# Four edits of order in a sigmoid-attention and SwiGLU kernel: a whole-row load, later transposes, scores ahead of FFN1, and visits moved by one tile

## The chip, the core and the metric

The kernel runs on one core of a Trainium2 chip. The core has five engines that run side by side and wait for each other through semaphores: TensorE (PE in the profile, with its weight loads shown apart as PEld), VectorE (DVE), ScalarE (ACT), GpSimd (POOL) and SyncE (SP). SP, ACT and POOL can each issue DMAs; a "q" behind an engine's name means its queue. The metric is the device time of one execution in microseconds, the median of several runs.

## The reference

```python
# q, k, v: (8 batches, 12 heads, 448 positions, 64)
scores = q @ k.T / sqrt(64) - log(448)
attn = 1 / (1 + exp(-scores)) @ v             # a sigmoid where a softmax would be
x = attn.transpose(0, 2, 1, 3).reshape(3584, 768)
g = x @ w_gate                                # (768, 1536)
out = (g * sigmoid(g) * (x @ w_val)) @ w_out  # (1536, 768), float32
```

## The kernel before, in words

**Attention.** The twelve heads of a batch are taken four at a time. Such a *quad* n (24 in all, three to a batch) has q and k, loaded as 128 rows that each hold, for two heads, 448 contiguous floats (7 chunks c of 64). They are cast to bf16 (`cast`, `cast_part`, lines 157 and 179) and transposed, on PE with a copy out of PSUM (`trans_pe`, lines 198 and 204) for quads 0 to 5 and by SP's DMA for the others. `chunk(n, c)` makes the scores of one chunk (four 64x64 matmuls, line 228) and their sigmoid on ACT (line 246, or 243 in two halves). When a quad's seven chunks are through, `pv(n)` multiplies by v (28 matmuls, line 260) and DVE copies the result out as two xT tiles (lines 269 and 274).

**Feed-forward.** FFN1 tile (b, f), one of 12 per batch, multiplies six xT pairs by w_gate and by w_val (12 matmuls, line 294). ACT takes the sigmoid of the gate half (line 312), DVE makes the product t1 (line 314) and the gated product hT (line 318). In tile f = 0 the last two pairs of both halves come last, since their xT tiles are the youngest; in every other tile the gate half is complete before the value half begins. For odd batches DVE also makes sums of hT tiles (line 377): `h_sums` puts them in a queue and `make_sums(2)` takes up to two behind each tile. FFN2 uses them in a product form with seven multiplications (`ffn2_group`, line 418) or plainly (`ffn2`, line 476).

**One ring of PSUM.** Scores, transposes, PV, FFN1 and FFN2 all draw their PSUM from one ring of four slots of two banks (`Banked`). The user four places on has to wait until the readers of a slot are done, bank by bank where the code says so.

**Order.** Everything is issued in the order of the program; no scheduler moves it. The first 30 us are written out by hand (from line 545 on): the loads, the chunks of quads 0 to 2, the transposes of quads 1 to 3 between them, PV 0 and 1, and an early start on FFN1 tiles (0, 0) to (0, 2) (`early`, from line 646), whose matmuls are put around chunks (2,5) and (2,6) and PV 2.

Quad 0's first loads are cut: ACT's queue brings chunks 0 and 1 of k, SP's queue chunks 0 to 3 of q, then chunks 4 to 6 of q, then chunks 2 to 6 of k (`load_part`, 320 KB in pieces of 1,280 bytes), then q and k of quads 1 to 3 whole (`load`, 448 KB each). POOL issues v and the weights, each behind the casts that stand ahead of it in its own order.

After that a list of *units* (FFN1 tiles, FFN2 groups, each with an estimated time) is walked. The scores of the later quads come in *visits*: groups of two, three or four chunks (four chunks, then three, for most quads). A four-chunk visit scores two chunks, then the PV of the quad that was completed before, then two more chunks. Each visit has a due time; when the estimated time of the walk has passed it, the visit goes ahead of the next unit. Hooks on a visit (`plan`) issue the casts and loads of quads further on, on POOL, and transposes, on SP.

Of the kernel before, what the change touches and what calls it, by code (L numbers as in the profile page):

```python
# [19 lines left out]
def kernel(  # L20
# [10 lines left out]
    nc = tc.nc  # L31
    ctx.enter_context(tc.manual_schedule())

    B, H, S, D = q.shape
    DM = H * D
    DFF = moe_w_gate.shape[1]
    C = S // D
# [100 lines left out]
    qkv_st = {}  # L138
    q16, v16, qT = {}, {}, {}

    def src_of(n, which):
        b, j = divmod(n, NJ)
        return (q, k, v)[which][b, 4 * j:4 * j + 4].rearrange("(h w) (p c) d -> (w p) h (c d)", w=2, c=C)

    def load_part(n, which, eng, lo, hi):

        st = osp.tile([128, DM], FP32, tag="osb", name=f"st{which}_{n}_{lo}")[:, :2 * (hi - lo) * D]
        st = st.rearrange("p (h x) -> p h x", h=2)
        eng.dma_start(out=st, in_=src_of(n, which)[:, :, lo * D:hi * D])
        qkv_st[(n, which, lo)] = st  # L150

    def cast_part(n, which, eng, lo, hi):
        st = qkv_st.pop((n, which, lo))
        t = htp.tile([128, 2, S], FP16, tag="hT", name=f"c16_{which}_{n}_{lo}").bitcast(BF16)
        t = t.rearrange("p b s -> p (b s)")[:, :(hi - lo) * 2 * D].rearrange("p (c h d) -> p c h d", h=2, d=D)
        q16[(n, which, lo)] = t
        (eng.copy if eng is nc.scalar else eng.tensor_copy)(
            out=t.rearrange("p c h d -> p h c d"), in_=st.rearrange("p h (c d) -> p h c d", d=D)
        )

    def load(n, which, eng=None):
        ramp = 2 * n + (1 - which)
        st = (
            stg.tile([128, 2, S], FP32, tag=f"R{ramp}", bufs=1, name=f"st{which}_{n}")
            if ramp < NR else stg.tile([128, 2, S], FP32, tag="stg", name=f"st{which}_{n}")
        )
        (eng or nc.sync).dma_start(out=st, in_=src_of(n, which))
        qkv_st[(n, which)] = st
# [23 lines left out]
    def trans_part(D2, bank, n, which, lo, hi, eng, d):  # L192

        t = q16.pop((n, which, lo))
        ps = D2.t.bitcast(BF16).rearrange("p w (c i) -> p w c i", c=8)
        for c in range(hi - lo):
            D2.write(
                nc.tensor.transpose(out=ps[:, bank, c, :], in_=t[:, c].rearrange("p h d -> p (h d)"), identity=idn),  # L198
                bank,
            )  # L200

        def copy():
            f = eng.copy if eng is nc.scalar else eng.tensor_copy
            D2.read(f(out=d, in_=ps[:, bank, :hi - lo, :]), bank)  # L204
            for c in range(lo, hi):
                qT[(n, which, c)] = d[:, c - lo]

        return copy

    def trans_pe(n):  # L210
        D2 = Banked()
        ds = [qkT.tile([128, C, 128], BF16, tag=f"T{w}", name=f"T{w}_{n}") for w in range(2)]
        for f in [trans_part(D2, w, n, w, 0, C, nc.vector, ds[w]) for w in range(2)]:
            f()
        qT[(n, 0)] = ds[0]
# [5 lines left out]
    def qk_tile(n, c):  # L221
        sd = Banked()
        sc = sd.t
        qt, kt = qT[(n, 0)], qT[(n, 1, c)]
        for w in range(2):
            for h2 in range(2):
                r = slice(h2 * 64, h2 * 64 + 64)
                nc.tensor.matmul(  # L228
                    out=sc[w * 64:(w + 1) * 64, h2, :S],
                    lhsT=kt[r, w * 64:(w + 1) * 64],  # L230
                    rhs=qt[r, :, w * 64:(w + 1) * 64],
                    start=True,
                    stop=True,
                )
        return sd
# [53 lines left out]
    def ffn1_mm(D, b, f, prs):  # L289
        cs = slice((f % FW) * 128, (f % FW) * 128 + 128)  # L290
        for i, w16 in enumerate((wg16, wv16)):
            for pr in prs:
                D.write(
                    nc.tensor.matmul(  # L294
                        out=D.t[:, i, :S], lhsT=w16[f // FW][:, pr, cs], rhs=xT[(b, pr)],
                        start=(pr == 0), stop=(pr == NP - 1),
                    ),
                    i,
                )

    def ffn1(b, f):
        D = Banked("f", made=(b // 2, f))
        for prs in (range(NP - 2), range(NP - 2, NP)) if f == 0 else (range(NP),):
            ffn1_mm(D, b, f, prs)
        ffn1_gate(D, b, f)
        if b % 2:
            h_sums(b // 2, f)
            make_sums(2)

    def ffn1_gate(D, b, f):  # L310
        s16 = tmp.tile([128, S], FP16, tag="s16", name="s16")
        D.read(nc.scalar.activation(out=s16, in_=D.t[:, 0, :S], func=SIGM), 0)  # L312
        t1 = tmp.tile([128, S], FP16, tag="t1", name="t1")
        D.read(nc.vector.tensor_tensor(out=t1, in0=D.t[:, 0, :S], in1=s16, op=MULT), 0)  # L314
        if b % 2 == 0:
            hT[(b // 2, f)] = htp.tile([128, 2, S], FP16, tag="hT", name=f"hT_{b // 2}_{f}")
        D.read(
            nc.vector.scalar_tensor_tensor(  # L318
                out=hT[(b // 2, f)][:, b % 2, :], in0=D.t[:, 1, :S], scalar=HSC, in1=t1, op0=MULT, op1=MULT
            ),  # L320
            1,
        )
# [24 lines left out]
        nc.vector.tensor_tensor(out=t, in0=a, in1=b, op=op)  # L347

    sumq = []

    def h_sums(pb, f):

        i = f // (2 * FW) * FW + f % FW
        if f // FW % 2 == 0:
            sumq.append((pb, i, f, 3))
        else:
            sumq.extend((pb, i, f - FW, kind) for kind in (1, 2, 4))

    def make_sums(most):
        for _ in range(min(most, len(sumq))):  # L360
            pb, i, f, kind = sumq.pop(0)
            h1 = hT[(pb, f)].rearrange("p b s -> p (b s)")
            a11, a21 = h1[:, :GT], h1[:, GT:2 * GT]
            if kind in (1, 4):
                h2 = hT[(pb, f + FW)].rearrange("p b s -> p (b s)")
                a12, a22 = h2[:, :GT], h2[:, GT:2 * GT]
            t = htp.tile([128, GT], FP16, tag=f"S{kind}_{i}", bufs=1, name=f"S{kind}_{pb}_{i}")
            hS[(pb, kind, i)] = t
            if kind == 1:
                a, b, op = a21, a22, ADD  # L370
            elif kind == 2:
                a, b, op = hS[(pb, 1, i)], a11, SUB
            elif kind == 3:
                a, b, op = a11, a21, SUB
            else:
                a, b, op = a12, hS[(pb, 2, i)], SUB
            nc.vector.tensor_tensor(out=t, in0=a, in1=b, op=op)
# [144 lines left out]
    visits = [tiles[:2], tiles[2:4]]  # L522
    for i in range(0, len(tiles), C):
        visits += [tiles[i:i + 4], tiles[i + 4:i + C]] if i else [tiles[4:C]]
    vtime = []
    for grp in visits:
        n, c = grp[0]
# [7 lines left out]
    def attn_step(group, pvs, how):  # L535
        for part in (group[:2], group[2:]):
            scs = [(n, c, qk_tile(n, c)) for n, c in part]
            rest = [pv(pvs.pop(0), how) for _ in range(len(pvs))]
            for i, (n, c, sc) in enumerate(scs):

                sig_tile(n, c, sc, split=len(group) == 4 and part[0] == group[0] and i == 1)
            for f in rest:
                f()
# [5 lines left out]
    QS, KS = 4, 2  # L549
    load_part(0, 1, nc.scalar, 0, KS)  # L550
    load_part(0, 0, nc.sync, 0, QS)
    load_part(0, 0, nc.sync, QS, C)
    load_part(0, 1, nc.sync, KS, C)
    for n, which in ((1, 0), (1, 1), (2, 0), (2, 1), (3, 0), (3, 1)):
        load(n, which)
    nc.scalar.activation(out=one.tile([128, 1], FP32, tag="tbl", name="tbl"), in_=sb_t, func=SIGM)
    for i in range(8):
# [37 lines left out]
    def chunk(n, c):  # L595
        sig_tile(n, c, qk_tile(n, c))
# [33 lines left out]
    w_load("g", 2)  # L630
    chunk(1, 5)
    chunk(1, 6)
    trans_pe(3)
    for c in range(3):
        chunk(2, c)
    pv(1)
    casts(4)
    w_load("v", 2)
# [7 lines left out]
    early = [Banked("f")]  # L646
    ffn1_mm(early[0], 0, 0, range(2))
    chunk(2, 5)
    ffn1_mm(early[0], 0, 0, range(2, NP - 2))
    chunk(2, 6)  # L650
    early.append(Banked("f"))
    ffn1_mm(early[1], 0, 1, range(NP - 2))
    pv(2, how=2, at=(k0 + 1) % 4)
# [32 lines left out]
    tcur = 3 * FU1  # L686
    vi = 0
    pend = []
    for dur, fn, args in units:
        if vi < len(visits) and tcur >= vtime[vi]:  # L690
            group = visits[vi]
            vi += 1
            pvs, pend = pend, []
            attn_step(group, pvs, 0 if fn is ffn1 else 1)
            for n, c in group:
                for act, of in plan.get((n, c), ()):
                    act(of)
                if c == C - 1:
                    pend.append(n)
            while post:  # L700
                trans_pe(post.pop())
        if pend and (
            fn is ffn1 and args[1] == 0 and (args[0], NP - 1) not in xT
            or vi == len(visits) and tcur >= vtime[-1] + 4.0
        ):
            for n in pend:
                pv(n)
            pend = []
        fn(*args)
        tcur += dur  # L710


# [28 lines left out]
```

## Time and profile before

| what | us |
|---|---|
| median of 6 runs | 417.58 (417.32 to 418.72) |
| the six runs | 418.72, 418.50, 417.32, 417.79, 417.35, 417.37 |
| the profiled execution, its own time | 418.72 |
| its span, first to last instruction | 416.9 |
| PE busy | 405.0 |
| DVE, ACT, POOL busy | 256.1, 214.0, 95.3 |

The page has PE busy for 97% of the span, and in the chain of work that ended last PE holds 90%. In rows of the timeline the first number is the start, the second the length, then come engine, line, operation, tiles and count, and in brackets how long the engine had been idle and what released it. The row of granted clocks gives, for each of 40 equal slices, the share of full speed that TensorE had. In the table by stretches each engine's busy time is followed by its number of instructions; the last three numbers of a row are the granted clock, the DMA share and GB/s.

### The profile page before, as it was taken

Reading aid. Unit: us, or ns where it says so; the run is one execution under the profiler, and the core shown is the slowest. Engines: PE = TensorE matmul, PEld = TensorE weight load, DVE = VectorE, ACT = ScalarE, POOL = GpSimd, SP = SyncE. Lnnn points to the kernel's source line nnn. Section 1 sums busy time; section 2 is a strip of 40 time slices with the busy share of each in tenths; the row PEclk is TensorE's granted clock in tenths of the full one; section 3 lists DMA queues with packets and bytes.
Section 4 is the critical chain, followed back from the end, with each engine's and each line's share of the span. In section 5 each row is a group of like instructions: output and inputs, shape, how many; then the busy total and the mean of one; then the engine's idle time right before and its main releaser. Section 6 shows DMA issues by size and latency. Waiting matters only on the chain.

```text
span 416.9 us, 7945 instructions
## 1 busy us (share of the span) xinstructions
PE 405.0 (97%) x3194; PEld 210.5 (50%) x3194; DVE 256.1 (61%) x472; ACT 214.0 (51%) x294; POOL 95.3 (23%) x125
## 2 busy tenths in 40 slices
PE   7699999999999999999999999999999999999995
PEld 3344545445555445445565445445555545555563
DVE  2636547678855546668654556568745447588653
ACT  5866895754354755755703955755715562222000
POOL 4628154343430334320030336200000000000000
PEclk9899999999999999999999999999999999999999
DMA  8999999978779988641274998630025500000125
GB/s 261 247 254 243 224 196 228 146 156 221 199 117 242 170 115 209 136 111 24 50 187 127 186 194 190 137 63 0 2 57 139 115 2 0 2 0 2 38 79 149
DMA packets 59845, 54.39 MB, mean 130 GB/s; under 512 B 35744, under 2 KB 53280, under 8 KB 59808
## 3 DMA queue, kind: packets, MB, share of 16 engines
q0 software_dynamic: 18880, 30.94, 35.3%
q1 hardware_dynamic: 40496, 22.62, 26.1%
q8 instruction: 25, 0.41, 0.4%
q10 hardware_dynamic: 432, 0.33, 0.3%
q14 instruction: 12, 0.10, 0.1%
HBM read 47.19 MB, written 11.01 MB: 140 GB/s over the span
## 4 chain that ended last, share of the span: by engine, by line
PE 90%; DMA 3%; DVE 3%; ACT 2%; issue 1%; SPq 0%; POOL 0%; DVEq 0%; ACTq 0%
PE ps_D L294 51%; PE ps_D L418 18%; PE ps_D L228 7%; PE ps_D L260 7%; PE ps_D L476 6%; DMA v<-in_v_dram 2%; ACT pt L246 1%; DMA st<-in_q_dram 1%; DVE t L314 1%; PE ps_D L198 1%; DVE T L204 1%; ACT s L312 1%; DVE xT L274 0%; DVE xT L269 0%; ACT pt L243 0%
## 5 line engine op out<-in xcount | busy, mean ns | idle before, releaser
L246 ACT ACTIVATE pt<-ps_D,sb_t 128x896 f16<-128x896 f32 x148 | 140.5, 1011 | 82.5 <-PE ps_D L228 76.7
L294 PE MATMUL ps_D<-xT,wg 128*128 128x448 f16 x576 | 126.9, 353 | 1.1 <-ACT pt L246 0.5
L294 PE MATMUL ps_D<-xT,wv 128*128 128x448 f16 x576 | 126.4, 352 | 0.0
L314 DVE TENSOR_TENSOR t<-ps_D,s 128x448 f16<-128x448 f32 x96 | 59.8, 623 | 76.1 <-ACT s L312 75.7
L312 ACT ACTIVATE s<-ps_D 128x448 f16<-128x448 f32 x96 | 52.7, 549 | 85.0 <-PE ps_D L294 73.1
L294 PEld LDWEIGHTS <-wg 128*128 128x128 f16 x576 | 53.5, 98 | 59.2 <-issue 13.7
L294 PEld LDWEIGHTS <-wv 128*128 128x128 f16 x576 | 56.3, 98 | 52.9 <-issue 0.3
L179 POOL CAST c<-st 128x896 bf16<-128x896 f32 x41 | 38.7, 953 | 135.9 <-DMA T<-c 60.6
L318 DVE SCALAR_TENSOR_TENSOR hT<-ps_D,t 128x448 f16<-128x448 f32 x96 | 60.0, 625 | 10.0
L228 PE MATMUL ps_D<-T,T 64*64 64x448 bf16 x644 | 44.3, 359 | 2.1 <-DVE xT L274 0.8
L260 PE MATMUL ps_D<-pt,v 64*64 64x448 f16 x672 | 37.1, 358 | 0.2 <-DMA v<-in_v_dram 0.2
L429 DVE TENSOR_SCALAR osb<-ps_D 128x384 f32<-128x384 f32 x43 | 24.0, 558 | 19.1 <-PE ps_D L418 18.1
L418 PEld LDWEIGHTS <-S 128*128 128x128 f16 x264 | 25.8, 98 | 17.1
L418 PE MATMUL ps_D<-wT,S 128*128 128x384 f16 x198 | 34.0, 326 | 0.0
L269 DVE CAST xT<-ps_D 128x448 f16<-128x448 f32 x24 | 15.0, 623 | 21.2 <-PE ps_D L260 15.6
L228 PEld LDWEIGHTS <-T 64*64 64x64 bf16 x644 | 15.2, 106 | 24.5 <-issue 18.9
L260 PEld LDWEIGHTS <-v 64*64 64x64 f16 x672 | 19.9, 109 | 14.1 <-issue 2.0
L435 DVE SCALAR_TENSOR_TENSOR osb<-ps_D,osb 128x384 f32<-128x384 f32 x33 | 18.4, 558 | 13.5 <-PE ps_D L418 13.5
L274 DVE CAST xT<-ps_D 64x448 f16<-64x448 f32 x42 | 26.1, 621 | 0.7
L418 PEld LDWEIGHTS <-hT 128*128 128x128 f16 x198 | 18.9, 98 | 14.2 <-issue 2.1
L172 POOL DMA_DIRECT2D v<-in_v_dram x24 | 17.6, 732 | 31.3 <-PE ps_D L228 27.2
L476 PE MATMUL ps_D<-wo,hT 128*128 128x384 f16 x144 | 24.2, 326 | 0.0
(45 smaller groups left out, 210.2 us busy)
## 6 DMA issues: line engine op xcount, KB each, us to landing
out_dram<-osb SPq DMA_DIRECT2D x52, 192.0 KB, 2.9
st<-in_q_dram POOLq DMA_DIRECT2D x20, 448.0 KB, 5.1
st<-in_k_dram POOLq DMA_DIRECT2D x20, 448.0 KB, 6.2
v<-in_v_dram POOLq DMA_DIRECT2D x24, 224.0 KB, 7.9
wg<-in_moe_w_gate_dram POOLq DMA_DIRECT2D x4, 576.0 KB, 12.1
wv<-in_moe_w_val_dram POOLq DMA_DIRECT2D x4, 576.0 KB, 12.8
wo<-in_moe_w_out_dram POOLq DMA_DIRECT2D x4, 576.0 KB, 11.1
st<-in_q_dram SPq DMA_DIRECT2D x3, 448.0 KB, 7.0
```

What stands on the lines that cost most here:

```text
L179: eng.tensor_copy(out=t.rearrange("p c h d -> p h c d"), in_=st.rearrange("p h (c d) -> p h c d", c=C))
L228: nc.tensor.matmul(out=sc[w * 64:(w + 1) * 64, h2, :S], lhsT=kt[r, w * 64:(w + 1) * 64], rhs=qt[r, :, w * 64:(w + 1) * 64], start=True, st ...
L246: nc.scalar.activation(out=pt, in_=sc[:, :, :S], func=SIGM, bias=sb_t, scale=qkscale)
L260: nc.tensor.matmul(out=P[g:g + 64, h2, :S], lhsT=vt[r, h2, c * D:(c + 1) * D], rhs=pt[r, h2, :], start=(c == 0), stop=(c == C - 1),)
L274: done = [nc.vector.tensor_copy(out=o, in_=i) for o, i in halves[how:]]
L294: nc.tensor.matmul(out=D.t[:, i, :S], lhsT=w16[f // FW][:, pr, cs], rhs=xT[(b, pr)], start=(pr == 0), stop=(pr == NP - 1),),
L312: D.read(nc.scalar.activation(out=s16, in_=D.t[:, 0, :S], func=SIGM), 0)
L314: D.read(nc.vector.tensor_tensor(out=t1, in0=D.t[:, 0, :S], in1=s16, op=MULT), 0)
L318: nc.vector.scalar_tensor_tensor(out=hT[(b // 2, f)][:, b % 2, :], in0=D.t[:, 1, :S], scalar=HSC, in1=t1, op0=MULT, op1=MULT),
L418: nc.tensor.matmul(out=D.t[:, bank, :hw], lhsT=l, rhs=B_(i), start=(first and i == 0), stop=(i == HF - 1), skip_group_check=True,),
L429: nc.vector.tensor_scalar(out=o, in0=D.t[:, bank, :hw], scalar1=HREC, scalar2=None, op0=MULT), bank
L476: nc.tensor.matmul(out=D.t[:, half, :hw], lhsT=h[:, m * 128:(m + 1) * 128], rhs=wo16[f // FW][:, f % FW, half * hw:(half + 1) * hw], start ...
```

## The change

1. The rest of quad 0's k is no longer a load of chunks 2 to 6. The whole k of quad 0 is loaded, all seven chunks in rows of 1,792 bytes, at the same place in SP's order, into a buffer of its own. Chunks 0 and 1 still come by ACT's queue too. `cast_part` takes its columns out of the whole tile.
2. `trans_pe(3)`, the transposes of quad 3 on PE, stands behind chunks (2,0) and (2,1) where it stood ahead of them.
3. Chunk (2,6) stands ahead of the second group of matmuls of the first early FFN1 tile, where it stood behind it.
4. In the walk over the units, a visit that is due waits for one more unit when the unit just done was FFN1 tile f = 0 of some batch.
5. The number of sums that DVE may make behind an FFN1 tile of an odd batch was two. It is one behind a tile that follows a visit with a PV, two behind one that follows another visit, and three elsewhere.

```diff
     def cast_part(n, which, eng, lo, hi):
-        st = qkv_st.pop((n, which, lo))
+        st = qkv_st.pop((n, which, lo)) if (n, which, lo) in qkv_st else qkv_st.pop((n, which))[:, :, lo * D:hi * D]
...
             h_sums(b // 2, f)
-            make_sums(2)
+            make_sums(sums_now[0])
...
     sumq = []
+    sums_now = [2]
...
     load_part(0, 0, nc.sync, QS, C)
-    load_part(0, 1, nc.sync, KS, C)
-    for n, which in ((1, 0), (1, 1), (2, 0), (2, 1), (3, 0), (3, 1)):
+    for n, which in ((0, 1), (1, 0), (1, 1), (2, 0), (2, 1), (3, 0), (3, 1)):
         load(n, which)
...
     chunk(1, 6)
+    chunk(2, 0)
+    chunk(2, 1)
     trans_pe(3)
-    for c in range(3):
-        chunk(2, c)
+    chunk(2, 2)
     pv(1)
...
     ffn1_mm(early[0], 0, 0, range(2))
     chunk(2, 5)
+    chunk(2, 6)
     ffn1_mm(early[0], 0, 0, range(2, NP - 2))
-    chunk(2, 6)
     early.append(Banked("f"))
...
+    was, was_args = ffn1, (0, 2)
     for dur, fn, args in units:
-        if vi < len(visits) and tcur >= vtime[vi]:
+        sums_now[0] = 3
+        if vi < len(visits) and tcur >= vtime[vi] and not (was is ffn1 and was_args[1] == 0):
             group = visits[vi]
             vi += 1
             pvs, pend = pend, []
+            sums_now[0] = 1 if pvs else 2
             attn_step(group, pvs, 0 if fn is ffn1 else 1)
...
         fn(*args)
+        was, was_args = fn, args
         tcur += dur
```

## The prediction

> **What bounds the kernel now.** I read the page first, then TensorE's (PE's) waits, the chain of waits through the first 60 us, and the timelines of PE and ACT around each edit.
>
> ```profile
> span 416.9 us, 7945 instructions
> PE 405.0 (97%) x3194; PEld 210.5 (50%) x3194; DVE 256.1 (61%) x472; ACT 214.0 (51%) x294; POOL 95.3 (23%) x125
> PEclk9899999999999999999999999999999999999999
> ```
>
> PE is busy in 405.0 of 416.9 us. The change keeps every matmul, so it can only give back part of the 12 us of idle time, most of it in the first 30 us, or add to it. There the chain reads:
>
> ```profile
> 5.32 8.07 DMA v<-in_v_dram
> ...
> 13.44 2.73 PE ps_D L260 x28
> ...
> 18.20 1.16 DVE T L204 x2
> 19.35 0.54 DVE c L179
> ...
> 21.82 1.54 PE ps_D L260 x28
> ...
> 25.36 0.38 PE ps_D L228 x4
> ```
>
> Quad 0's v lands at 13.39; its PV runs; then DVE sets the pace (xT copies, T copies of quad 2, casts and T copies of quad 3), until quad 1's PV (21.82) and the scores of chunk (2,5) (25.36). From 31.88 on PE hardly stops. That first PV took 2.7 us and the second 1.5, both 28 matmuls; the table by stretches tells why (the number before the DMA share is the granted clock):
>
> ```profile
> 9.04:12.45 3.41, 1.86 (x30) 1.24 (x30) 2.40 (x4) 3.41 (x5) 3.41 (x5) 1.00 1.11 308
> 12.45:15.87 3.42, 3.23 (x36) 1.34 (x38) 0.99 (x1) 3.42 (x4) 3.01 (x4) 0.50 1.20 289
> ```
>
> Half a clock for 3.4 us, after a stretch in which PE was busy for 1.86 us.
>
> Later, PE loses time only around visits (the groups of score tiles between FFN1 tiles). PE's timeline, three places:
>
> ```profile
> 51.30 0.76 PE L228 MATMUL ps_D<-T,T 64*64 64x448 bf16 x12
> 52.15 1.29 PE L294 MATMUL ps_D<-xT,wg 128*128 128x448 f16 x6
> ...
> 56.41 0.57 PE L228 MATMUL ps_D<-T,T 64*64 64x448 bf16 x8
> ...
> 232.16 0.76 PE L228 MATMUL ps_D<-T,T 64*64 64x448 bf16 x12
> 233.15 1.29 PE L294 MATMUL ps_D<-xT,wg 128*128 128x448 f16 x6 [0.22 <-DVE t L314]
> ...
> 237.28 0.57 PE L228 MATMUL ps_D<-T,T 64*64 64x448 bf16 x8
> ...
> 327.77 0.76 PE L228 MATMUL ps_D<-T,T 64*64 64x448 bf16 x12
> ...
> 332.88 0.57 PE L228 MATMUL ps_D<-T,T 64*64 64x448 bf16 x8
> ```
>
> Each x12 row is a visit of three chunks, each x8 row the second half of a four-chunk visit with a PV, with one FFN1 tile between the two visits. The distances are 5.11, 5.12 and 5.11 us. That equality is the key to part four.
>
> **Part one, k of quad 0 in whole rows.** The load grows from 320 to 448 KB. The DMAs moved 349 GB/s from 5.62 to 9.04, so 131 KB are 0.38 us for all behind it on SP's queue. It landed 4.3 us after its issue at 1.75, at 6.05; DVE's cast starts at 6.22, so it slips by at most 0.25, and the third chunk's scores from 7.98 to 8.23. ACT works without a gap from 6.79, 0.91 us a chunk, and takes the third at 8.61; scores precede their sigmoid by 0.43 (6.36 to 6.79), so 8.66: 0.05 late, hidden by ACT's idle 0.55 before 16.43. q and k of quads 1 to 3 come 0.38 later and are cast long before use: k of quad 3 is cast at 19.8, quad 1's T is wanted by ACT at 13.0 and scored at 11.5. What could count is v of quad 0, on POOL's queue, issued at 5.32 behind a cast that waits only for q's second part, which is ahead of k in SP's queue: not later. Its landing moves by 0 to 0.38. The Trainium skill (DMA: Bandwidth & Descriptors, "Queues, rings and completion order") says that each DMA engine takes turns between queue rows packet by packet; by that SP's longer row costs v nothing, by the row of 349 GB/s 0.38. No view here shows the turns, but v's landing in the middle of SP's six loads fits the first better; I take +0.10. The columns read twice cost no engine anything: the cast still takes 5 of 7 chunks.
>
> **Part two, quad 3's transposes behind chunks (2,0) and (2,1).** Before, PE stood 1.15 us at 19.94 for DVE's cast, and ACT idled:
>
> ```profile
> 21.49 6.54 ACT L246 ACTIVATE pt<-ps_D,sb_t 128x896 f16<-128x896 f32 x7 [0.94 <-ACT pt L246]
> ```
>
> Moved up, the two scores need quad 2's T copies (done 19.36) and free ring slots (free by then), so they run at 19.4 to 19.8 inside that stall, and the transposes still start at 19.94. ACT goes on at 20.56. But PV 1 now takes the slot of (2,0), not that of the transposes: it waits for that sigmoid, 20.56 + 0.93 + 0.05 = 21.55, in place of the T copies' end, 21.78. It gains 0.27, not 0.94; xT copies and chunk (2,5), which takes PV 1's slot, follow: -0.27.
>
> This holds with half a clock before it. The skill (TensorE: Matmul & The Clock Gate, Part 1) says that the gate judges by free-running windows of about 3.4 us, so that the same kernel can meet it at another phase. The six times (four in 417.32 to 417.79, two at 418.50 and 418.72) suit that, and the profiled one is the 418.72. Without the half clock PV 0 ends 1.17 sooner (2.69 against 1.52). Then DVE's chain ends in T copies at about 20.35; after the change ACT's unbroken row from 6.79 binds, fifteen sigmoids of 0.914 to 20.50. Part two then costs 0.10 and gains nothing, and ACT hides part one's 0.10. By the row -0.27; by the rule +0.10.
>
> **Part three, chunk (2,6) ahead of the early FFN1 matmuls.** From (2,5) at 25.36 to PV 2 at 28.46 are 3.10 us: chunk, 4 matmuls, chunk, 8 matmuls. Two chunks together precede FFN1 by 0.51 (36.32 to 36.83); twelve matmuls in a row take 2.27, and PV follows 0.10 later: 2.88. So -0.22. Its slot was last used by (2,3), whose sigmoid is done by 24.2. PV 2 needs (2,6)'s sigmoid by about 28: it comes sooner.
>
> **Part four, visits.** The planner now puts off a visit when the previous unit was tile 0 of a batch. The two orders differ at four places: tiles (12,4-6) and (19,0-3) go behind FFN1 (3,1) and (5,1); (16,4-6) and the next visit go behind (4,1) and (4,2); (23,0-3) goes behind (6,1). Tile 0 gets its gate half late (its last two pairs come last), so the ring slot is freed late: 0.29 lost at 168.81 (0.98 after the visit's start, ordinary 0.69), 0.30 at 233.15. But the 5.11 us above is a second limit: three sigmoids, then the lone tile's sigmoid, product and gated product must end before the four-chunk visit can reuse that tile's slot. PE's own work over the same stretch is 0.69 + 2.36 + 0.40 + 1.33 = 4.78, so 0.33 is lost wherever one tile lies between such visits, as at 52.15 and 56.41 (0.16 each) without any tile 0.
> - (3,x): the visits come to lie one tile apart, before two: 0.29 goes, 0.33 comes: +0.04.
> - (4,x): one tile before and after: 0.30 + 0.04 becomes 0.33: -0.01.
> - (6,x): one tile becomes two: 0.30 at 332.88 goes: -0.30.
> - (5,x): no stall before (268.66), none after: 0.
> Together -0.27. The moved visits issue POOL's casts and loads for quads two and three on, and SP's transposes, one tile (2.3 us) later; a transpose lands 4.5 us after issue and the next user is two visits on: 0.
>
> **Part five, sums.** DVE makes up to three instead of two behind a tile, after a visit two or, with a PV, one. Each is 0.36; their number is the same. A third sum can only delay the next tile's products. The tightest place, hT at 96.61 + 0.62 = 97.23 for PE at 97.67, leaves 0.43: covered. Bounds: -0.10 (the 0.09 lost at 80.91, behind sums) to +0.30. I take 0.
>
> **Sum.** With the half clock: 0.10 - 0.27 - 0.22 - 0.27 = -0.66 from the profiled 418.72 (span 416.9, 1.8 outside): 418.06. Without: 0.10 - 0.22 - 0.27 = -0.39. The median, 417.58, is 1.14 below the profiled run and most runs are near it, so I use the second: **417.2**.
>
> **Rivals.** (a) The idle times are worth their face value: 0.94 of ACT, 0.22, and 0.29 + 0.34 + 0.30 with no new stall: -2.09 at most; with PV 1's 0.27 instead, -1.42: 416.2. For: PE waits are listed for just these. Against: the 5.11 us. (b) Slower: the clock gate. Part one leaves PE emptier from 6 to 9 us; if a 3.4 us window falls under the 1.86 us of work that preceded half speed (15.87 to 19.28 held 2.10), another PV runs at half speed: +1.17, less 0.39: 418.4. It decides when the median execution meets it; that the two extra chunks fill 19.4 to 19.8 speaks against. (c) v lands 0.38 later, DVE's third sum stalls once or twice: gain eaten, 417.5.
>
> **How the numbers follow.** 0.2% is 0.84 us, about what a measurement of this kernel can tell from no change. Forecast 0.45 (own range 416.8 to 417.6), (a) 0.28, (b) 0.17, (c) 0.10. Faster: (a) plus the forecast's lower tail, 0.32; slower 0.17; same 0.51. The range reaches (a) and most of (b): 416.2 to 418.3.
>
> **What would show it.** ACT's idle 0.94 before (2,0) gone, PV 1 released by ACT, not DVE; (2,5) to PV 2 in 2.9 us; a new wait in the four-chunk visit behind (3,2), 5.11 after the visit before; no wait behind (6,1). Wrong if that distance shrinks, or if half-clock stretches differ in number.

## The result, and the profile after

Measured side by side, the changed kernel takes 418.9 us (417.81 to 421.23, 35 runs) where the kernel before takes 418.16 (417.24 to 420.43, 72 runs): a ratio of 1.002, interval 1.0012 to 1.0027, so it is slower by some 0.8 us. The forecast was a gain of about 0.4; its base, 417.58, was the median of six executions of the kernel before, and the median of all 72 lies 0.6 higher. One execution each of two experiments below (e11 and e13) took some 702 us at a granted clock of 0.56 and is left out of the ratios; e13's was the profiled one, so there is no profile of part one alone. The changed kernel's profiled execution took 418.57, with a span of 416.8; its page (length of the span, PE's busy time, granted clock by slices):

```profile
span 416.8 us, 7942 instructions
PE 405.0 (97%) x3194; PEld 210.5 (51%) x3194; DVE 259.6 (62%) x472; ACT 213.7 (51%) x294; POOL 94.9 (23%) x125
PEclk8999999999999999999999999999999999999998
```

PE does the same work in the same time. DVE does the same 472 instructions, but is busy for 259.6 us where it was 256.1: 3.5 us more for an unchanged list of work. The 96 sums make up 2.5 of it (34.8 us before, 37.3 now). That is the line to follow. The half clock is still there, in another slice. The chain of waits in the first 30 us of the changed kernel:

```profile
8.65 4.61 ACT pt L246 x5
...
13.30 1.54 PE ps_D L260 x28
...
19.34 1.10 ACT pt L246
...
20.49 1.54 PE ps_D L260 x28
...
24.09 0.57 PE ps_D L228 x8
24.66 2.38 PE ps_D L294 x12
27.04 1.48 PE ps_D L260 x28
```

PV 1 (20.49) is now released by ACT, and (2,5) to PV 2 (24.09 to 27.04) is 2.95 us, as forecast. ACT's idle 0.94 is gone too:

```profile
6.72 17.50 ACT L246 ACTIVATE pt<-ps_D,sb_t 128x896 f16<-128x896 f32 x19 [1.17 <-PE ps_D L228]
```

Here parts two and three did what they were to do. The half clock, in the table by stretches:

```profile
4.90:8.30 3.40, 1.99 (x26) 1.14 (x30) 1.77 (x4) 1.95 (x3) 1.75 (x3) 1.00 1.04 365
8.30:11.70 3.40, 3.40 (x34) 1.95 (x26) 1.91 (x3) 3.38 (x5) 3.40 (x5) 0.50 1.11 327
```

It fell on scores and transposes from 8.3 to 11.7, where it fell on PV 0 before. Then PE's timeline of the changed kernel, at the places where it loses time:

```profile
87.87 1.30 PE L294 MATMUL ps_D<-xT,wg 128*128 128x448 f16 x6 [0.28 <-DVE t L314]
...
99.97 1.30 PE L477 MATMUL ps_D<-wo,hT 128*128 128x384 f16 x7 [0.55 <-DVE xT L274]
```

```profile
169.63 0.76 PE L228 MATMUL ps_D<-T,T 64*64 64x448 bf16 x12
...
174.75 0.57 PE L228 MATMUL ps_D<-T,T 64*64 64x448 bf16 x8
```

```profile
299.84 0.57 PE L228 MATMUL ps_D<-T,T 64*64 64x448 bf16 x8 [0.28 <-DVE hT L318]
```

The visits behaved as forecast: 169.63 to 174.75 is 5.12 us again (0.31 lost), near 239 another 0.38, and nothing behind tile (6,1). Losses are counted from here on as the distance between the starts of two groups of matmuls less what that distance is where nothing waits; the idle time in brackets is smaller, since the ends of matmuls overlap. So counted, the four places of part four lost 0.92 in the profile before and lose 0.69 now: -0.23, forecast -0.27. New are three losses that no step of the forecast has: 0.34 at 87.87, at least 0.5 at 99.97 (it starts 1.84 behind the matmuls before it, in the kernel before 1.14; some records are missing there) and 0.45 at 299.84. All three are waits for DVE. What DVE and POOL did just before the first two:

```profile
85.93 0.36 DVE L378 TENSOR_TENSOR S<-S,hT 128x384 f16<-128x384 f16 x1
86.32 0.97 DVE L378 TENSOR_TENSOR S<-hT,S 128x384 f16<-128x384 f16 x1
87.21 0.61 DVE L314 TENSOR_TENSOR t<-ps_D,s 128x448 f16<-128x448 f32 x1
...
96.66 1.07 DVE L378 TENSOR_TENSOR S<-S,hT 128x384 f16<-128x384 f16 x1
97.75 0.36 DVE L378 TENSOR_TENSOR S<-hT,S 128x384 f16<-128x384 f16 x1
...
98.66 1.26 DVE L274 CAST xT<-ps_D 64x448 f16<-64x448 f32 x2
```

```profile
85.98 1.10 POOL L179 CAST c<-st 128x896 bf16<-128x896 f32 x1 [0.29 <-DMA st<-in_k_dram]
...
96.58 0.94 POOL L179 CAST c<-st 128x896 bf16<-128x896 f32 x1 [4.26 <-DMA st<-in_k_dram]
```

A sum that takes 0.36 us in the row at 97.75 took 0.97 and 1.07 where a cast of POOL (85.98 to 87.08, 96.58 to 97.52) had begun just before it, and ended 0.2 us after that cast. Three sums in a row then take 1.8 us instead of 1.1, and what DVE does behind them comes too late for PE: the product t at 87.21, and in the second place the xT copies, which end at 99.92.

### The profile page after: what moved, and what is told of

Read it like the earlier page. It is cut to its first block, busy times and chain, and to the rows that moved or that the text cites. A ratio compares the mean times of both kernels' runs of the same rounds, so it can differ in the third digit from the quotient of the medians.

```text
span 416.8 us, 7942 instructions
## 1 busy us (share of the span) xinstructions
PE 405.0 (97%) x3194; PEld 210.5 (51%) x3194; DVE 259.6 (62%) x472; ACT 213.7 (51%) x294; POOL 94.9 (23%) x125
## 4 chain that ended last, share of the span: by engine, by line
PE 85%; DVE 6%; ACT 5%; issue 2%; DMA 1%; SPq 0%; DVEq 0%; ACTq 0%
PE ps_D L294 47%; PE ps_D L419 18%; PE ps_D L228 7%; PE ps_D L260 6%; PE ps_D L477 6%; ACT pt L246 3%; DVE t L314 1%; DVE S L378 1%; DVE hT L318 1%; DMA st<-in_k_dram 1%; ACT s L312 1%; DVE xT L274 1%; DVE xT L269 1%; PE ps_D L198 1%; ACT pt L243 0%
## 5 line engine op out<-in xcount | busy, mean ns | idle before, releaser
L260 PE MATMUL ps_D<-pt,v 64*64 64x448 f16 x672 | 36.0, 349 | 0.6 <-ACT pt L246 0.6
```

The source lines that it names most:

```text
L260: nc.tensor.matmul(out=P[g:g + 64, h2, :S], lhsT=vt[r, h2, c * D:(c + 1) * D], rhs=pt[r, h2, :], start=(c == 0), stop=(c == C - 1),)
```

## The experiments

Each kernel was timed in five rounds against the kernel before on the same chip; a ratio is to that, with a 95% interval.

**The parts, alone and together.** e1 has parts one to four with `make_sums(2)`; e2, part five alone; e3, part four alone; e4, parts one to three alone.

> Parts one to four of the change with the fixed two sums of before. Sums theory (the third sum behind a tile, made longer where it meets a cast on POOL, is what costs time): the stalls at 87.9, 100.0 and 299.8 us of the changed kernel (0.35 + 0.61 + 0.45 = 1.4 us) go, so it runs about 0.5 us faster than before, 1.3 us faster than the changed kernel. Visits theory (moving the visits by a tile is what costs, through the work that hangs on them): it stays 0.8 us slower than before. Ramp theory (the larger k load is what costs): likewise 0.8 us slower.

> The kernel before with part five alone, one to three sums behind a tile. Sums theory: 1.0 to 1.4 us slower than before, with PE stalls near a visit of batches 1, 3 or 5 and sums of about 1 us beside POOL casts. Visits and ramp theories: no change, within 0.2 us.

> The kernel before with part four alone. Sums and ramp theories: 0.23 us faster than before, from the stalls in both traces (0.29 + 0.33 + 0.31 goes, 0.31 + 0.38 comes). Visits theory: 0.8 us slower.

> The kernel before with parts one to three, the first 30 us, alone. Sums and visits theories: 0.1 to 0.4 us faster than before. Ramp theory: 0.8 us or more slower.

| kernel | median us | ratio |
|---|---|---|
| e1 parts 1 to 4, two sums | 417.63 | 0.9995 (0.9986 to 1.0003) |
| e2 part 5 | 417.99 | 1.0006 (0.9998 to 1.0015) |
| e3 part 4 | 417.49 | 0.9997 (0.9985 to 1.0009) |
| e4 parts 1 to 3 | 417.85 | 1.0002 (0.9992 to 1.0011) |

Without the sum rule no kernel is shown slower. With the sum rule alone the ratio was too near 1 to say, where 1.0 to 1.4 us had been expected; in e2's profiled execution PE lost 0.67 at 88.66.

**Where the rule costs.** e5 is the changed kernel again; e6 keeps the rule in batch 1 only, where POOL's casts lie beside the sums; e7 keeps it in batches 3, 5 and 7; e8 has parts four and five.

```diff
-            make_sums(sums_now[0])
+            make_sums(sums_now[0] if b == 1 else 2)     # e6
+            make_sums(2 if b == 1 else sums_now[0])     # e7
```

> The changed kernel once more, beside the next three on the same chip. 0.8 us slower than before; a mid-run stretch at half clock in more than half of its executions (the kernels with parts one to three showed a mean clock of 0.998 or more in 21 of 64 executions, those without in 62 of 87).

> The changed kernel with the one-to-three rule in batch 1 only, two sums in batches 3, 5 and 7. Collision theory (a sum that runs beside a POOL cast takes about 1 us, and POOL's casts lie beside sums only in batch 1): nearly as slow as the changed kernel, 0.6 us or more slower than before. Lateness theory (three sums in a row are late for a visit in any batch): about half of the loss stays.

> The changed kernel with two sums in batch 1 and the one-to-three rule in batches 3, 5 and 7. Collision theory: as fast as the version with two sums throughout, 0.1 to 0.3 us faster than before. Lateness theory: half of the loss stays, 0.3 us or more slower than before, with stalls at visits of batches 3 and 5.

> The kernel before with parts four and five, without the edits of the first 30 us. If visits and sums together make the loss: 0.8 us slower than before. If the sums cost more only where the first 30 us are changed: 0 to 0.2 us slower, as the sums alone less what the visits give.

| kernel | median us | ratio |
|---|---|---|
| e5 the changed kernel | 418.92 | 1.0027 (1.0018 to 1.0037) |
| e6 rule in batch 1 | 418.70 | 1.0025 (1.0014 to 1.0035) |
| e7 rule in batches 3, 5, 7 | 418.58 | 1.0022 (1.0013 to 1.0031) |
| e8 parts 4 and 5 | 418.53 | 1.0021 (1.0011 to 1.0031) |

Halving the rule did not halve its cost. The theory that only casts beside sums cost time fails with e7, which has two sums wherever casts lie beside them and is slow all the same. In the profiles, e6 loses 0.56 in batch 1, e7 0.45 near 299; each also carries what other parts cost. e8 shows that the first 30 us aren't needed for a loss, though its profiled execution, the fastest of its 22 (417.32), shows next to none of it. Since every kernel of this set with the rule was slow and those of the first set without it were not, but on another chip, the control came next.

**The control on one chip.** The same four kernels as marks: e9 is e1 again, e10 the changed kernel, e11 the visits, e12 the sums.

> Parts one to four with two sums behind every tile, beside the changed kernel, the visits alone and the sums alone on one chip. If the sum rule is what costs: 0.9990 to 1.0003 of the kernel before here, and 1.002 or more for the changed kernel. If the earlier runs of this kernel were good only because of the chip that they met: 1.0015 or more here too.

> The changed kernel, unchanged, as the mark for the other three: 1.002 to 1.003 by either theory.

> Part four alone. If the sum rule is what costs: 0.9990 to 1.0000. If the moved visits are: 1.0010 to 1.0025, as for the visits with the sums.

> Part five alone. If the sum rule costs by itself: 1.0010 to 1.0025, where the first run had 1.0006. If it costs only together with the moved visits: 1.0000 to 1.0008.

| kernel | median us | ratio |
|---|---|---|
| e9 parts 1 to 4, two sums | 418.15 | 1.0002 (0.9991 to 1.0013) |
| e10 the changed kernel | 419.05 | 1.0023 (1.0012 to 1.0035) |
| e11 part 4 | 417.76 | 0.9992 (0.9981 to 1.0003) |
| e12 part 5 | 418.94 | 1.0019 (1.0009 to 1.0029) |

The sum rule costs by itself, and taking it out of the changed kernel brings 0.9 us back. e10's profiled execution shows the mechanism at its largest (DVE, then POOL, then PE):

```profile
95.35 0.36 DVE L378 TENSOR_TENSOR S<-hT,hT 128x384 f16<-128x384 f16 x1
95.74 0.97 DVE L378 TENSOR_TENSOR S<-S,hT 128x384 f16<-128x384 f16 x1
96.74 1.09 DVE L378 TENSOR_TENSOR S<-hT,S 128x384 f16<-128x384 f16 x1
97.76 0.61 DVE L314 TENSOR_TENSOR t<-ps_D,s 128x448 f16<-128x448 f32 x1
```

```profile
95.53 0.97 POOL L179 CAST c<-st 128x896 bf16<-128x896 f32 x1 [1.76 <-DMA st<-in_q_dram]
96.69 0.94 POOL L179 CAST c<-st 128x896 bf16<-128x896 f32 x1 [0.19 <-DMA st<-in_k_dram]
```

```profile
99.15 0.57 PE L228 MATMUL ps_D<-T,T 64*64 64x448 bf16 x8 [1.05 <-DVE hT L318]
```

Two casts, two sums held, and the hT that PE needs comes over 1 us late. The casts wait for q and k to land (the releasers in the POOL rows), and where they fall against the sums differs from execution to execution: so does the loss in batch 1, from nothing in e8's profile to 1.2 us here.

**Casts put beside sums; part one alone; without part one.** e16 is the changed kernel with six more casts of POOL in batch 3, each of a finished hT tile into a spare tile:

```diff
             make_sums(sums_now[0])
+            if b == 3 and f % 2:
+                nc.gpsimd.tensor_copy(out=spare, in_=hT[(b // 2, f)])
```

e13 is the kernel before with part one only; e14 has parts two to four; e15 is e14 in which, from quad 12 on, a visit also waits while only one FFN1 tile has passed since the last visit:

```diff
-        if vi < len(visits) and tcur >= vtime[vi] and not (was is ffn1 and was_args[1] == 0):
+        if vi < len(visits) and tcur >= vtime[vi] and not (was is ffn1 and was_args[1] == 0) and not (lone == 1 and visits[vi][0][0] > 11):
+            lone = 0
...
+        lone += 1 if fn is ffn1 else 2
```

> Part one alone. If the whole-row k is what empties PE from 5 to 8 us and so brings half clock: at most 40% of executions with a granted clock of 0.998 or more, and 1.0003 to 1.0012. If it is parts two and three: 55% or more, and 0.9995 to 1.0004.

> Parts two, three and four, without part one and with two sums. If part one brings the half clock: 55% or more of executions at 0.998 or more, and 0.9982 to 0.9994 (visits -0.23, part three -0.2). If it is parts two and three: 40% or less, and 0.9995 to 1.0003.

> As the one before, and from quad 12 on a visit also waits for a second FFN1 tile behind the last one. If the lone tile between two visits is the limit: the losses of 0.31 near 175 and 0.38 near 239 go, 0.69 in all, so 0.0016 below the one before. If the ring slot is late for another reason, the stalls move on with the visits and the two are level.

> The changed kernel with one cast of GpSimd more behind the gated product of every second tile of batch 3 (a copy of the finished hT into a spare tile, six in all; the result is as before). If a sum is held while GpSimd reads memory beside it: each of the six makes one sum of 0.36 take 0.8 to 1.1, three sums and the products of the next tile come late, and PE loses 1 us or more in batch 3: 0.0025 or more above the changed kernel. If the long sums of batch 1 have another cause: sums of 0.36 there and 0.0000 to 0.0005 more.

| kernel | median us | ratio | granted clock 0.998 or more |
|---|---|---|---|
| e13 part 1 | 418.45 | 1.0012 (1.0002 to 1.0021) | 3 of 22 runs |
| e14 parts 2 to 4 | 417.00 | 0.9983 (0.9975 to 0.9990) | 12 of 15 |
| e15 and two tiles | 416.35 | 0.9959 (0.9947 to 0.9971) | 5 of 5 |
| e16 changed, more casts | 419.39 | 1.0030 (1.0016 to 1.0043) | 4 of 10 |

e16, DVE and then POOL in batch 3, where no profile of the unaltered casts has a long sum:

```profile
183.98 0.35 DVE L381 TENSOR_TENSOR S<-S,hT 128x384 f16<-128x384 f16 x1
184.36 0.98 DVE L381 TENSOR_TENSOR S<-hT,S 128x384 f16<-128x384 f16 x1
185.26 1.08 DVE L381 TENSOR_TENSOR S<-hT,hT 128x384 f16<-128x384 f16 x1
```

```profile
184.20 0.93 POOL L311 CAST spare<-hT 128x896 bf16<-128x896 f16 x1 [3.11 <-DVE hT L321]
185.08 2.06 POOL L180 CAST c<-st 128x896 bf16<-128x896 f32 x2
```

A cast put there makes the long sum there. Three of the six added casts began just before a sum, and all three held it (0.98 to 1.09 us); the other three met none. The expected price was missed, though: PE lost only 0.23 in batch 3 (at 192.73), and the held sums mostly fell where PE wanted nothing for a while. The hold is shown; whether it costs depends on the place.

Part one alone is slower and leaves few executions at full clock (a granted clock of 0.998 or more; one stretch of 3.4 us at half speed takes 0.004 off the mean of a span of 417): 3 of 22, where the kernel before has 23 of 40 on the same chip and e14 12 of 15. Both are as the first branch of its expectation had it. Taken over all the experiments, 36 of 160 executions of kernels with part one were at full clock, 103 of 155 of the altered kernels without it, and 168 of 263 of the kernel before. On the four chips the full-clock executions of the kernel before were 0.45 to 1.17 us shorter in the median than its others.

e15 settles the lone tile. PE around the first of the two places, e14 and then e15:

```profile
168.50 0.76 PE L228 MATMUL ps_D<-T,T 64*64 64x448 bf16 x12
...
171.97 1.49 PE L260 MATMUL ps_D<-pt,v 64*64 64x448 f16 x28
173.61 0.57 PE L228 MATMUL ps_D<-T,T 64*64 64x448 bf16 x8
```

```profile
168.76 0.76 PE L228 MATMUL ps_D<-T,T 64*64 64x448 bf16 x12
...
174.50 1.49 PE L260 MATMUL ps_D<-pt,v 64*64 64x448 f16 x28
175.83 0.55 PE L228 MATMUL ps_D<-T,T 64*64 64x448 bf16 x8
```

With one tile between, PV to the last scores is 1.64 us (171.97 to 173.61); with two it is 1.33, PE's own pace. Both losses are gone and did not come back elsewhere: 0.65 between the medians, 0.69 expected (the ratios, with only five executions of e15, give 1.0).

**Which half of the rule.** e17 puts the whole sum rule on e15, e18 the rule with two in place of three:

```diff
-        sums_now[0] = 3
+        sums_now[0] = 2     # e18
```

> The kernel without part one and with a second tile between visits, now with the whole sum rule of the change. If the third sum costs wherever a cast of GpSimd holds it: 0.0012 to 0.0022 above the same kernel with two sums (0.9959), so 0.9971 to 0.9981. If the rule costs only next to the other edits: 0.9955 to 0.9965.

> As the one before, with at most two sums behind a tile in place of three (one behind a visit with a PV, as in the change). If the third sum is what costs: level with the kernel of two sums everywhere, 0.9955 to 0.9963. If the sums held back and made up at the end of a batch cost: 0.9968 or more.

e17: 417.71, ratio 0.9997 (0.9986 to 1.0009). e18: 416.73, 0.9976 (0.9961 to 0.9990). The third sum costs 0.98 us between the medians, on one chip and with nothing else different. With 22 and 11 executions the two intervals still overlap a little, so the size is rough; e10 against e9 gave 0.9 for the whole rule. e17 came out slower than both its expectations. In its profile it loses 0.73 in batch 1 and 0.45 in batch 5. DVE, POOL and PE at the first, then DVE and PE at the second:

```profile
86.19 1.13 DVE L378 TENSOR_TENSOR S<-S,hT 128x384 f16<-128x384 f16 x1
87.35 0.36 DVE L378 TENSOR_TENSOR S<-hT,S 128x384 f16<-128x384 f16 x1
87.63 0.62 DVE L314 TENSOR_TENSOR t<-ps_D,s 128x448 f16<-128x448 f32 x1
```

```profile
86.17 0.93 POOL L179 CAST c<-st 128x896 bf16<-128x896 f32 x1 [0.23 <-DMA st<-in_k_dram]
```

```profile
88.30 1.30 PE L294 MATMUL ps_D<-xT,wg 128*128 128x448 f16 x6 [0.66 <-DVE t L314]
```

```profile
296.37 0.63 DVE L318 SCALAR_TENSOR_TENSOR hT<-ps_D,t 128x448 f16<-128x448 f32 x1 [0.46 <-DVE t L314]
```

```profile
299.10 0.57 PE L228 MATMUL ps_D<-T,T 64*64 64x448 bf16 x8 [0.28 <-DVE hT L318]
```

e18's profiled execution has neither loss. It came out between its two expectations, 0.9976 for 0.9955 to 0.9963; its interval meets e15's, which ran on another chip, so whether the held-back sums cost something of their own stays open.

## Why the prediction was wrong

**Part five is the step that failed.** It said "A third sum can only delay the next tile's products. The tightest place, hT at 96.61 + 0.62 = 97.23 for PE at 97.67, leaves 0.43: covered", with 0.36 for a sum, and bounds of -0.10 to +0.30. The runs show 0.98 (e17 against e18) and ratios of 1.0006 and 1.0019 for the rule alone. A sum isn't always 0.36, and it can delay the xT copies as well as the products. In 19 profiles (all but e13's), 63 of the 72 sums that began with a POOL cast still under way took over 0.44 us (median of the 72: 0.89), and each of the 63 ended 0.20 to 0.21 after its cast; none of the 1,709 that met no cast took more than 0.361, and none of the 43 during which a cast began took more than 0.36. The kernel before has held sums too, but with two sums there was mostly room: in the ten profiles without the third sum in batch 1 PE loses some 0.1 there on average, in the nine with it some 0.7. A third sum uses 0.36 of the 0.43, and a hold of 0.6 no longer fits. The profile before carried the warning, one sum of 1.08 beside two casts of POOL; pricing the edit from the usual row passed over it:

```profile
89.42 1.08 DVE L377 TENSOR_TENSOR S<-hT 128x384 f16<-128x384 f16 x1
```

```profile
89.15 2.14 POOL L179 CAST c<-st 128x896 bf16<-128x896 f32 x2 [12.03 <-DMA st<-in_q_dram]
```

The Trainium skill (SBUF — State Buffer, "SBUF: two separate sides") states the rule: a DVE instruction with two SBUF inputs and a GpSimd instruction that reads SBUF contend for one port pair, which the first to start holds to its end. The rows agree. The held sums end a fixed time after the cast, wherever in it they began. The cast is held in its turn: the one at 85.98 began 0.05 behind a sum and took 1.10, where 559 of the 564 casts behind 68 us that began beside no sum took 0.93 to 0.94. And DVE's work with an input in PSUM isn't held: of 171 products t and 179 hT that began under a cast, none took more than 0.63, their usual length.

The loss near 299 is not of this kind, and its cause stays open: no cast is near, and the profile names only t as what hT waited for at 296.37, although t ended 0.46 before. It is 0.45 in the profiles of e5, e7, e10, e16, e17 and the changed kernel, 0.10 in e2 and e12, which have the third sum without the moved visits, but also 0.10 in e8, which has both, and nothing in e18 without the third sum. So what the third sum costs in batch 1 is explained (0.73 in e17's profile); why hT starts late in batch 5 isn't.

**Part one was mis-sized through the clock.** Its times were nearly right: the third chunk's sigmoid starts at 8.65 for a forecast of 8.66. Its +0.10 for v did not come: PV 0 starts at 13.30 (13.44 before), behind ACT and not behind v. But the sum was made for an execution without half clock, because most executions before were like that, and part one changes just this: 22% of executions with it at full clock, 66% without. That is rival (b)'s outcome, with part one as the cause it named, at 0.5 us in the median (e13) and not the +1.17 that it gave the median execution. How an emptier PE and the clock are linked isn't settled: the changed kernel's profile has 1.99 us of PE work in the 3.40 before half speed, while e11's, which stays at full speed there, has less in the same stretch:

```profile
4.90:8.30 3.40, 1.70 (x26) 0.89 (x28) 1.77 (x4) 2.16 (x3) 1.53 (x3) 1.00 1.01 370
```

**Parts two and three were right in their mechanism.** PV 1 is released by ACT; (2,5) to PV 2 takes 2.95 for a forecast of 2.9. With part one away, e14's ratio is 0.0009 and 0.0014 below those of the two runs of the visits alone, on other chips: 0.4 to 0.6 us, where 0.12 was forecast. The profiles at full clock show less: PV 0 to PV 2 takes 13.66 in e14 and e15, 13.85 to 13.99 in e3, e8 and e11, a gain of 0.2 to 0.3; the rest may be the clock or the chip. Of part two's term without half clock, the 20.35 for the T copies does not follow from the numbers beside it (21.78 less 1.17 is 20.61), and its +0.10 did not come: PV 0 to PV 1 takes 7.18 in e14 and e15, 7.21 to 7.35 in e3, e8 and e11.

**Part four was right.** -0.23 in the profile for -0.27; alone 0.9997 and 0.9992. The second limit, 5.11 us over a lone tile, holds, and e15 shows what removing it is worth.

Together: some -0.2 for the visits, -0.2 to -0.6 for parts two and three, +0.5 for part one and +0.8 to 1.0 for the sum rule make +0.5 to +1.1, around the +0.8 measured; no run shows that they add so simply. Rival (a) fell with the 5.12 us; rival (c) had "DVE's third sum stalls once or twice" inside a case that ended level with before, where it is the larger part of the result.

## What to carry to other kernels

Before giving an engine more work in a gap, look at the longest row of that kind of instruction, not the usual one, and at what ran beside it: here sums of DVE with both inputs in SBUF and casts of GpSimd held each other up, and a gap that took two such sums did not take three. A change to the first microseconds is to be judged over many executions, by how often the clock drops, and not by one profile. Where two visits lie the same distance apart at several places, count PE's own work between them: what is left over is the gain to be had. Here that was e15's second tile, which with parts two to four and two sums makes a kernel of 416.35 us, where the kernel before takes 417.79 on the same chip.

## What was not expected of the hardware

A DVE sum of 0.36 us becomes 0.97 to 1.13 when a GpSimd cast of 0.93 begins just before it: it ends some 0.2 after the cast, and in e16 two in a row were held, one behind each cast. And one load of 448 KB in place of one of 320 KB, issued in the first 2 us, changes how often the granted clock falls below 0.998: from a third of the executions to more than three quarters.
